# A long convolution by matrix steps: rows regrouped by residue, two steps of the second half in small tiles, their exchanges through DRAM

## The chip, the core and the metric

The program runs on one core of a Trainium2 chip. The core has five engines that run side by side, each working through its own instructions in order: PE (matrix products; the loading of its weights is listed apart as PEld), DVE (element by element), ACT (functions and casts), POOL (small work) and SP, which here only issues transfers. The transfers themselves are carried by 16 DMA engines. The metric is the time of one execution in device microseconds (us); lower is better.

## The reference

All matrices are bf16; S = 2048 rows, D = 512 columns. The core of it:

```
x  = q
k_shift[t] = k[t]*s0 + k[t-1]*s1 + k[t-2]*s2 + k[t-3]*s3      (per column)
kv = k_shift * v
y  = causal convolution of kv with ssm_k over the 2048 rows    (by a Fourier transform of length 4096)
h  = x + layernorm(x) * (y + kv * ssm_D)
z  = layernorm(h)
g  = gelu(layernorm(z) @ w1), its four quarters of columns moved by -1, +1, -2, +2 rows
x1 = z + g @ w2
out = h + x1 + gelu(layernorm(x1) @ w3) @ w4                   (hidden width 1792)
```

## The kernel before

**Layout.** Row t of the sequence is t = 1024 s + 8 p + b: half s, partition p (0 to 127), block b (0 to 7). A block is a 128 x 512 tile, a pair is two blocks. So a load of q or v reads, for each of 128 partitions, one contiguous piece of several rows.

**The convolution.** The two halves of kv are called A0 and A1, those of the filter F0 and F1. Each goes through a transform in two steps. Step 1 (tasks S1, L397) multiplies 128 x 512 blocks by a 128 x 32 table `f1`; of each table only a quarter of the rows is nonzero (the mask `mk`, L238), so that one product picks out one residue of the row number. There are four b by two hp tasks of 8 products for each of the four signals. The result in PSUM is cast to SBUF (E1, L266), and an exchange (X, L412) moves it between partitions, SBUF to SBUF: 8 transfers of 256 KB for each signal. Step 2 (S2, L420) is followed by a cast (E2, L266); for F1 the place of the cast is taken by a fold on DVE (L432), which joins F1's spectrum with F0's (16 instructions). Products of spectra (P, L481) go through the inverse's first step (I2, L493, 32 x 32 tiles), a cast (EV, L266), an exchange (XI, L503, four transfers of 512 KB for each half) and the inverse's last step (I1, L511), with a table `f2` that is masked in the same way. The first half needs A0 F0; the second A0 F1 + A1 F0. The shift of k is done by products with diagonal tiles (K, L449), the gating with v on DVE (KV, L457).

**After the convolution.** H (L619) forms h from I1, HS takes its moments, uw, rr and hn turn them into scales, hb (L653, L655) normalizes. hb is transposed per pair either on PE (LT, L671, with a copy TE) or through DRAM by a transfer that transposes (LT L664, TE L666; `BYDMA` lists the pairs). W (L700) is w1, U the gelu (L704), X2 (L729) w2 on shifted blocks, S (L732) x1, R (L736) the residual. Then come ux, r1, xn and lb, the transpose (LX, EX), M (L781, w3, seven tasks of 16 products a pair), G (L785, gelu), O (L793, w4, 14 products a block), Z (L795, the sum into `obt`, two slots) and OUT (L797).

**Order.** `Plan` records some 800 tasks; nothing is scheduled on the chip. The string `ORDER` lists them by number, engine letter and buffer slots, and each engine runs its tasks in that order; so a task that waits holds all that stands behind it on its engine. Every transfer is issued by SP. The built program uses eight completion semaphores for them in turn: a transfer waits until the one eight places before it has landed. SP issues 125 transfers. All but one have 128, 64 or 32 as the outermost count on both sides; the one is `Lsd` (L280), a single row.

**Memory.** `fxs` (the filter) lies in `r_h`, q in `r_q`, v in `r_v`; `r_x`, `r_y`, `r_f0`, `r_f1`, `r_a0` hold spectra and later the hidden activations.

Of the kernel before, what the change touches and what calls it, by code (L numbers as in the profile page):

```python
# [9 lines left out]
P = 128  # L10
S = 2048
D = 512
F = 1792
DC = D // P
FC = F // P
NB = 8
XW = 258
KW = NB * 129 + 4
# [13 lines left out]
029P7 004S 030P 031V 067P01 069P23 005S 033A 068A 041V 042G 070A 003S 037V 008S 036V 040V 063P45 002S 064A 065P67 066A 059P01 046V 099P30 043V 000S  # L32
060A 047V 001S 007S 006S 034G 038A 032V 044V 035G 105P2 010S 100V 091P71 061P01 039A 055P45 106V 009S 048A 021S 092V 056A 340V 101P6 102V 103P3 104V
045A 062A 097P2 098V 015S 022S 342V 023S 343V 093P7 057P45 019S 053G 119P01 058A 120A 095P6 049G 050V 121P23 051A 094V 054G 017S 122A 115P45 117P01
118A 024S 078S 096V 111P67 113P23 114A 116V 107P45 112V 109P01 110A 108V 074S 088P6723 090V 089A 345V 077S 071S 073S 075S 085P0145 087V 079P6723 127S
086A 130S 128S 123S 081A 344V 219P10 220V 080A 131P2345 133A 132V 124S 134P6701 135V 136A 072S 076S 082P2345 083A 084A 223P1 125S 144V0 129S 137P6723
020S 227P01 138A 143V1 146V2 147V3 139A 145P45670 148P 231P3 224V 149M 150A 228V 346V 152V0 012S 126S 187P01 189P45 188A 190A 153V1 155V2 018S 232V
014S 195P67 011S 183P01 196V 185P23 184A 186V 013S 191P45 192A 151S 025S 156V3 140P6701 142A 141A 154P23451 157P 347V 225P1 016S 197P67 158M 159A 198A
221P0 201S 161V0 162V1 226V 199S 200S 193P23 194A 341V 163P45670 202S 348G 165V2 164V3 166P 168A 167A 222V 160S 233P1 204S 229P0 170V0 171V1 174V2
239P23 173V3 203S 349G 172P45671 234V 240A 175P 230V 177A 176V 350G 354G0 207P0123 052A 208V 206S 209V 235P67 216P4501 217V 236A 351G1 241P67 242A  # L40
271V0 169S 339G 205S 243P23 244A 178S 179P54 218V 237P67 238A 355V 360G0 247P23 336S 352V 357G1 335S 180P10 361V 358V 356A 338S 245P67 248A 353A 375V
249P45 181P03 246A 366G0 367V 250A 182P12 255S 363G1 251S 364V 376G 377V 362A 359A 372G0 365A 252S 213P4567 215V 378A0 369G1 379P30 381A1 373V 374A
026S 027S 382P2 380A 370V 272V1 259P6701 254S 383A 260A 388G 389G 390G 214V 274V2 275V3 258S 386P3 371A 387A 210P4567 212V 211V 256S 261A 273P01230
391A0 392P71 394A1 395P6 276P 277V0 413G 414G 393A 396A 368A 278V1 262P4567 281V2 415G 401G 253S 402G 403G 280V3 263A 028S 279P 257S 282P 283M 284A
416V0 399P5 400A 384P4 385A 418S 417V1 419S 286V0 268P0123 420S0 264V 269A 397P7 398A 287V1 289V2 270V 404G0 290V3 265P4501 266A 288P23671 291P 406S
423P5 405A1 292V0 424A 293V1 296V2 267A 294P 421P4 295V3 297P 422A 285S 298A 407S 513P5 302V0 301V1 303P01230 304V2 408S0 305V3 306P 299A 509P4 514V
307V0 308V1 411P5 515A 409P7 510V 511A 310V2 311V3 309P 312P 412A 317V0 410A 521P7 313A 300S 314A 517P6 316V1 320V2 319V3 318P01451 522V 321P 322V0
525P3 337S 573G 574G 575G 579A0 576A1 323V1 325V2 577P70 578A 529P2 580P7 315S 326V3 523A 324P 581A 518V 519A 602G 603G 604G 605G0 327P 329A 328A
582P70 588P6 594P5 430V 431V 429V 584P4 426V 585A 330S 583A 425V 592P1 593A 586P0 427V 589A 587A 428V 432V 433V 590P4 591A 526V 530V 434G 527V 606A1
331P76 332P43 333P21 531A 435V 439G0 595A 516V 440V 599P5 436A1 441A 437V 445G0 442G1 630V 438V 446V 451A0 443V 608S 596P0 631G 632G 607S 609S0 600V0  # L50
601S 460G 461G 334P37 444A 447A 473G 452V 448A1 633V0 635S 610P60 614P1 634V1 611A 616P5 620P6 449V 612P4 450V 457G0 453V 454A1 618P2 615A 462G 466A0
613A 617A 458V 622P7 636S 637S1 638P10 644P5 623A 455V 463V1 464P70 465A 621A 459V 619A 524V 640P4 456V 467P3 645A 646P7 474G 475V 477G1 479S 468V
469P6 471P5 497V 520V 498G 624P3 476A0 499V 478S 528V 480S0 472A 470A 500A1 625V0 502S 533P6 534V 485G 501A0 503S 504S1 537P5 538V 648P3 650P6 649A
539A 535V 483P5 484A 486G 487V 642P3 643A 489V0 491S 481P2 647A 488G1 627P5 658G 659G 660G 482A 512V 597V1 532V 662A0 507P7 490S 492S0 641A 661A1 663S
508A 505P4 495P0 493P7 506A 541P4 545P3 626S 546V 639A 494A 496A 553P7 557P2 561P3 651A 549P6 547A 554V 542V 543A 742V 743G 562V 563A 598S 555A 558V
744V 745A1 550V 569P4 565P7 566V 664S 665S0 666P30 667A 674P2 675A 678P6 652P7 655P3 560V 746V0 748S 628V0 672P5 564V 629S 747S 749S1 676P2 570V 571V
750P40 751A 668P1 669A 548V 756P0 551V 757A 686G 687G 688V 677A 690V0 692S 752P4 753A 689V1 552V 673A 670P1 671A 559V 760P2 761A 762P5 691S 714V 715G
716V 754P4 718G0 717V1 693S0 758P2 759A 694P10 696P0 653V0 654S 704P7 719S 568V 679A 705A 680P2 700P7 540V 695A 536V 763A 702P6 698P5 755A 767P4 720S
656V1 567V 657S 699A 701A 770G 771G 697A 706P7 721S1 722P50 772G 773G0 730P3 774G1 731A 556V 776S 724P1 725A 544V 775S 683P0 684V0 777S0 734P3 703A
764P6 707A 778P70 784P1 685S 728P0 785A 735A 765V0 766S 711P6 681V1 782P1 572V 783A 712V0 713S 682S 732P3 733A 726P6 729A 768V0 769S 727A 708P2 709V1  # L60
710S 723A 788P6 789A 739P5 740V0 741S 790P6 786P4 791A 787A 780P5 781A 736P6 737V0 738S 779A 792P7 793V1 794S 795P6 796V0 797S
# [3 lines left out]
class Plan:  # L65
# [4 lines left out]
    def add(self, name, opts, fn, deps=(), take=(), drop=(), size=0, mode=0, port="", mate=None):  # L70
        n = len(self.t)
        t = dict(mate=mate, n=n, name=name, opts=opts, fn=fn, deps=set(), take=list(take), drop=[], size=size, mode=mode, port=port)
        for d in deps:
            t["deps"].add(self.by[d])
        for d, part, *kind in drop:
            m = self.by[d]
            t["deps"].add(m)
            t["drop"].append((m, kind[0] if kind else self.t[m]["take"][0][0], part))
        self.by[name] = n
        self.t.append(t)  # L80
# [20 lines left out]
def body(ctx, tc, fx, kt, q, v, sd, w1, w2, w3, w4, out):  # L101
# [13 lines left out]
    def view(raw_, lo, n, pat, **kw):  # L115
        return raw_[:, lo:lo + n].rearrange(pat, **kw)


    G = 8192
    GS = FC * 256  # L120
    r_q, r_f0, r_f1, r_a0, r_x, r_y, r_v = (raw(n, G) for n in ("r_q", "r_f0", "r_f1", "r_a0", "r_x", "r_y", "r_v"))
    r_k = raw("r_k", 2 * DC * KW)
    r_h = raw("r_h", DC * NB * XW)
    r_kv = raw("r_kv", 8 * D)
    r_p = raw("r_p", 4 * 2 * D)
    r_vs = raw("r_vs", 2 * 4 * D)
    r_dg = raw("r_dg", DC * 4 * P)
# [718 lines left out]
```

## Time and profile before

| | |
|---|---|
| timed executions | 220.81 and 221.84 us, median 221.32 |
| the profiled execution, first to last instruction | 221.2 us |
| PE, DVE, ACT, POOL busy | 200.6, 145.3, 134.9, 67.3 us |
| transfers | 34.47 MB, mean 156 GB/s |
| the first I1 of the first half (L511) starts | 56.2 us |
| the first step 2 of A1 (L420 on r_x) starts | 68.7 us |
| last product ends, last sum (Z) ends | 217.5, 218.2 us |

A table row here is a view's own number, or a start that stands in the timeline of one engine. Busy shares are means over the whole run: PE is busy 91% of the span, but what bounds the first third is not what bounds the rest, so the prediction reads the profile by stage. The page's own span and the median of the two timed executions differ by 0.1 us.

### The profile page before, as it was taken

To read this page: it belongs to the slowest core of one execution; us is meant where nothing else is said; L and a number is where in the kernel's file an instruction comes from. 1 tells how busy PE (TensorE), PEld (TensorE's weight loads), DVE (VectorE), ACT (ScalarE), POOL (GpSimd) and SP (SyncE) were. 2 spreads that over 40 slices of the span, in tenths; PEclk is the share of its full clock that TensorE was granted. 3 is DMA by queue.
4 is the path that set the end of the run, shared out by engine and by line. 5 is a ranking of instruction groups with operands and counts; after the bars stand their busy time and mean duration, and the time that the engine had idled before them with its cause. 6 is when DMAs were issued, how large, how long until landed. Compare 5 with 4: busy or idle time off the path is not lost.

```text
span 221.2 us, 5913 instructions
## 1 busy us (share of the span) xinstructions
PE 200.6 (91%) x2372; PEld 118.7 (54%) x2372; DVE 145.3 (66%) x320; ACT 134.9 (61%) x214; POOL 67.3 (30%) x187
## 2 busy tenths in 40 slices
PE   6889578996867799999999999999999999999993
PEld 4454234451223255558548958746588666665641
DVE  7898989999499899899899348059765001312121
ACT  4799889988498979687956646655063323123400
POOL 7342000093276680234685345003125000000000
PEclk9999999999695899999999999999999999999998
DMA  6996798869927535973234154341415402111001
GB/s 193 363 394 271 286 291 318 309 244 307 426 115 268 187 83 160 269 303 98 50 74 95 27 113 102 89 104 46 91 32 142 98 2 45 47 50 47 24 24 47
DMA packets 35996, 34.47 MB, mean 156 GB/s; under 512 B 26753, under 2 KB 28802, under 8 KB 35714
## 3 DMA queue, kind: packets, MB, share of 16 engines
q1 hardware_dynamic: 35970, 34.11, 48.6%
q8 instruction: 18, 0.29, 0.6%
q14 instruction: 8, 0.07, 0.1%
HBM read 13.13 MB, written 5.24 MB: 83 GB/s over the span
## 4 chain that ended last, share of the span: by engine, by line
PE 67%; DMA 11%; SPq 6%; ACT 6%; DVE 5%; issue 2%; POOL 0%; DVEq 0%
PE ps L781 22%; PE ps L793 22%; PE ps L729 6%; PE ps L700 5%; PE ps L493 4%; SPq L412 4%; DMA r_h<-in_fx_dram 3%; SPq L275 3%; DMA r_k<-in_kt_dram 3%; DMA r_x<-r_y 3%; PE ps L511 3%; DVE r_f L432 2%; PE ps L397 2%; ACT r_y L266 2%; DMA r_f<-r_y 2%
## 5 line engine op out<-in xcount | busy, mean ns | idle before, releaser
L781 PE MATMUL ps<-r_dg,r_k 128*128 128x256 bf16 x448 | 51.4, 273 | 0.0
L781 PEld LDWEIGHTS <-r_k 128*128 128x128 bf16 x448 | 43.6, 98 | 7.8 <-issue 0.7
L785 ACT ACTIVATE r_f<-ps 128x512 bf16<-128x512 f32 x26 | 14.9, 598 | 27.8 <-PE ps L781 27.8
L793 PE MATMUL ps<-w4s,r_f 128*128 128x512 bf16 x104 | 24.1, 379 | 0.0
L481 DVE TENSOR_TENSOR r_p<-r_a,r_f 128x1024 bf16<-128x1024 bf16 x32 | 20.8, 694 | 1.0 <-PE ps L493 0.9
L266 ACT CAST r_y<-ps 128x1024 bf16<-128x1024 f32 x19 | 18.6, 1022 | 4.6 <-PE ps L397 4.1
L493 PE MATMUL ps<-r_p,ttab 32*32 32x512 bf16 x768 | 15.8, 379 | 1.4 <-ACT r_x L266 0.6
L700 PE MATMUL ps<-hnT,r_v 128*128 128x256 bf16 x128 | 16.5, 281 | 0.5 <-DMA hnT<-dhb 0.5
L795 DVE TENSOR_TENSOR r_kv<-ps,r_v 128x512 bf16<-128x512 f32 x5 | 3.4, 686 | 20.5 <-PE ps L793 20.5
L795 DVE TENSOR_TENSOR r_kv<-ps,r_a 128x512 bf16<-128x512 f32 x6 | 4.2, 692 | 19.3 <-PE ps L793 17.3
L449 PE MATMUL ps<-r_dg,r_k 128*128 128x256 bf16 (+3 forms) x112 | 15.8, 288 | 1.0 <-ACT r_dg L314 0.5
L785 ACT ACTIVATE r_x<-ps 128x512 bf16<-128x512 f32 x16 | 9.2, 599 | 12.2 <-PE ps L781 12.2
L793 PEld LDWEIGHTS <-r_f 128*128 128x128 bf16 x104 | 10.2, 98 | 11.8
L266 ACT CAST r_vs<-ps 128x1024 bf16<-128x1024 f32 (+1 forms) x12 | 14.3, 1228 | 2.4 <-PE ps L493 1.9
L700 PEld LDWEIGHTS <-r_v 128*128 128x128 bf16 x128 | 12.5, 100 | 5.1 <-issue 2.0
L793 PE MATMUL ps<-w4s,r_x 128*128 128x512 bf16 x64 | 15.1, 379 | 0.0
L729 PE MATMUL ps<-r_v,r_h 128*128 128x512 bf16 x64 | 15.0, 380 | 0.0
L449 PEld LDWEIGHTS <-r_k 128*128 128x128 bf16 x112 | 9.5, 98 | 8.9 <-issue 4.6
L266 ACT CAST r_x<-ps 128x1024 bf16<-128x1024 f32 x14 | 13.7, 1017 | 0.7 <-PE ps L397 0.4
L397 PEld LDWEIGHTS <-f 128*32 128x32 bf16 x256 | 6.2, 99 | 12.6 <-issue 7.3
L493 PEld LDWEIGHTS <-ttab 32*32 32x32 bf16 x768 | 8.3, 88 | 8.7 <-issue 6.0
L793 PE MATMUL ps<-w4s,r_kv 128*128 128x512 bf16 x56 | 12.6, 379 | 0.0
(180 smaller groups left out, 343.8 us busy)
## 6 DMA issues: line engine op xcount, KB each, us to landing
r_k<-in_kt_dram SPq DMA_DIRECT2D x8, 259.0 KB, 5.6
r_h<-in_fx_dram SPq DMA_DIRECT2D x8, 256.0 KB, 4.9
r_v<-in_v_dram SPq DMA_DIRECT2D x4, 512.0 KB, 6.2
r_q<-in_q_dram SPq DMA_DIRECT2D x8, 256.0 KB, 6.4
r_f<-r_x SPq DMA_DIRECT2D x8, 256.0 KB, 3.0
r_a<-r_y SPq DMA_DIRECT2D x8, 256.0 KB, 3.5
r_x<-r_vs SPq DMA_DIRECT2D x4, 512.0 KB, 3.5
r_f<-r_y SPq DMA_DIRECT2D x8, 256.0 KB, 4.0
```

Of the source, the lines that this page charges most:

```text
L266: (act.copy if e in "AM" else on[e].tensor_copy)(o, i)
L397: nc.tensor.matmul(ps[32 * j:32 * j + 32, sl[hh], :], lhsT=f1t[:, 4 * t + 2 * hp + hh, :], rhs=src(2 * b + b0), start=True, stop=True)
L412: nc.sync.dma_start(z2[sig][g:P:2, kl, :, :], z1[sig][kl:P:4, 2 * g:2 * g + 2, :, :])
L449: nc.tensor.matmul(o[:, (d + j0) * P:(d + j1 + 1) * P], lhsT=kT[s][c][:, bb, x:x + P], rhs=diag[:, c, j0:j1 + 1, :].rearrange("p j x -> p ...
L481: on[e].tensor_tensor(out=prs[:, sl[0], :, :], in0=sp[a][:, kl, t, :, :], in1=gv, op=MUL)
L493: nc.tensor.matmul(ps[c:c + 32, bk[h], :], lhsT=ttab[32 * h:32 * h + 32, 2 * kl + t, 2 if x else xx, 32 * b0:32 * b0 + 32], rhs=prs[32 * h ...
L700: nc.tensor.matmul(ps[:, sl[0], j * 256:(j + 1) * 256], lhsT=w1s[:, k, m * P:(m + 1) * P], rhs=hnT[:, k_, k, :], start=(k == 0), stop=(k = ...
L729: nc.tensor.matmul(ps[:, sl[0], :], lhsT=h1T[:, m, bb, x:x + P], rhs=w2s[:, m, :], start=(m == 0), stop=(m == DC - 1))
L781: nc.tensor.matmul(ps[:, sl[0], j * 256:(j + 1) * 256], lhsT=w3s[:, k, fc * P:(fc + 1) * P], rhs=lnT[:, k_, k, :], start=(k == 0), stop=(k ...
L785: act.activation(gb(gi, 2 * fp, 2), ps[:, got(("M", s, p, fp))[0], :].rearrange("p (j x) -> p j x", j=2), ACT.Gelu_apprx_tanh)
L793: nc.tensor.matmul(ps[:, sl[0], :], lhsT=gb(gi, fc)[:, 0, (b % 2) * P:(b % 2 + 1) * P], rhs=w4s[:, fc, :], start=(fc == 0), stop=(fc == FC ...
L795: add(("Z", s, b), {V: 0.61}, lambda e, sl, b=b: vec.tensor_tensor(out=obt[sl[0]], in0=ps[:, got(("O", s, b))[0], :], in1=h_sb[s][:, b, :] ...
```

## The change

The rows keep their blocks, but within a block the 128 rows are regrouped by residue: partition 32 r + n now holds what partition 4 n + r held. Loads of q and v and the stores of the output therefore read and write DRAM with outermost count 4 and 32 rows under each. k and the filter are regrouped on the host.

With the residues apart, step 1 of F1 and A1 no longer needs a mask: a residue is 32 partitions, and the product is one of 32 x 32 tiles (`step1r`), four tasks of 16 products for A1, and four of 32 for F1, which takes over the fold: it adds F0 times a turned table `s1g`. The eight tasks of step 1 of F0 and A0 stay masked. The exchanges of F1 and A1 go through DRAM: 16 writes of 128 KB each (XW, outermost count 8) and then 4 reads of 512 KB (XR), the first of which waits for all 16 writes. The second half's last inverse step is unmasked too (64 x 32 tiles, `f2u`), and its exchange also goes through DRAM: 16 writes XIW and 4 reads XIR. SP issues 159 transfers.

The memory plan is new: F1's filter lies in the second half of `r_q`, so the q loads of the second half wait for F1's step 1, and so do w1 and w2; h overwrites v's place; Z writes in place, without slots; six buffers for hidden activations in place of four; shifted rows across the ends of a block get spare columns (`HO`, `KO`) and small copies (exa, exb, ed0, ed1, edge0, edge1). Pairs (0,2) and (0,3) of hb are transposed on PE. The first half's pairs go into M and O in the order (0,1), (0,2), (0,0), (0,3), and ORDER is new: two pairs' M stand among the second half's I2, and the second half's I1 stands behind the O of those two.

```diff
-KW = NB * 129 + 4
+KW = 5 * P + 3 * 160 + 4
...
 ORDER = """
...
-    for i in range(2):
-        for j in range(2):
-            vec.tensor_scalar(out=f1[:, :, i, :, j, :], in0=s1.rearrange("p (a c k) -> p a c k", a=8, c=2),
-                              scalar1=mk[:, 2 * i + j:2 * i + j + 1], scalar2=None, op0=MUL)
+    for r in range(4):
+        vec.tensor_scalar(out=f1[:, :, :, :, r, :].rearrange("p h t c k -> p (t c) h k"), in0=s1[:].rearrange("p t c (k h) -> p (t c) h k", h=4),
+                          scalar1=mk[:, r:r + 1], scalar2=None, op0=MUL)
...
-    v_r = v.rearrange("o (s p b) d -> p (o s) b d", s=2, b=NB)
-    q_r = q.rearrange("o (s p b) d -> p (o s) b d", s=2, b=NB)
-    o_r = out.rearrange("o (s p b) d -> p (o s) b d", s=2, b=NB)
+    v_r = v.rearrange("o (s n r b) d -> r n (o s) b d", s=2, r=4, b=NB)
+    q_r = q.rearrange("o (s n r b) d -> r n (o s) b d", s=2, r=4, b=NB)
+    o_r = out.rearrange("o (s n r b) d -> r n (o s) b d", s=2, r=4, b=NB)
...
-            load(("Lq", s, g), q_sb[:, s, 2 * g:2 * g + 2, :], q_r[:, s, 2 * g:2 * g + 2, :], size=310)
+            load(("Lq", s, g), q_sb[:, s, 2 * g:2 * g + 2, :], q_r[:, :, s, 2 * g:2 * g + 2, :], [("S1", "F1", b, 0) for b in range(4)] if s else [], size=310)
...
+    def step1r(b, srcs):
+        def f(e, sl):
+            for i, (src, tab) in enumerate(srcs):
+                for r in range(4):
+                    for t in range(2):
+                        for b0 in range(2):
+                            j = 2 * t + b0
+                            nc.tensor.matmul(ps[32 * j:32 * j + 32, sl[r], :], lhsT=tab[32 * r:32 * r + 32, 32 * t:32 * t + 32], rhs=src(2 * b + b0)[32 * r:32 * r + 32, :],
+                                             start=(i == 0), stop=(i == len(srcs) - 1))
+        return f
...
+    def forward1r(sig, srcs, sdeps, zdeps, xdeps, sdrop=None):
+        zd = scr.tile([P, 16, D], BF16, name="zd" + sig)
+        zx = zd[:].rearrange("(a r x) k d -> x r a k d", a=8, r=4)
+        for b in range(4):
+            n = ("S1", sig, b, 0)
+            add(n, {PEc: 0.23 * len(srcs)}, step1r(b, srcs), sdeps(b) + zdeps(b), take=[("ps", -2)], drop=[sdrop(b)] if sdrop else [], mode=3)
+            for hp in range(2):
...
+                def f(e, s, b=b, hp=hp):
+                    for r in (2 * hp, 2 * hp + 1):
+                        nc.sync.dma_start(zx[2 * (b % 2) + b // 2, r], z1[sig][:, b, r, :])
+                add(("XW", sig, b, hp), {SP: 0.85}, f, [("E1", sig, b, hp)], size=310)
+        for kl in range(4):
+            add(("XR", sig, kl), {SP: 0.6}, lambda e, s, kl=kl: nc.sync.dma_start(z2[sig][:, kl, :, :], zd[:, 4 * kl:4 * kl + 4, :]),
+                [("XW", sig, b, hp) for b in range(4) for hp in range(2)] + list(xdeps), size=620)
...
-                if sig == "F1":
-                    def fold(e, sl, n=n, kl=kl, t=t):
-                        for r, op in ((0, SUB), (1, ADD)):
-                            vec.tensor_tensor(out=sp[sig][:, kl, t, r, :], in0=ps[:, got(n)[2 * t + r], :], in1=sp["F0"][:, kl, t, 1 - r, :], op=op)
-                    add(("E2", sig, kl, t), {V: 1.2}, fold, [("E2", "F0", kl, t)], drop=[(n, t)])
-                    continue
...
+    wd = scr.tile([P, 16, D], BF16, name="wd")
+    wx = wd[:].rearrange("(a h k) n d -> k h a n d", a=8, h=4)
...
+            if s:
+                for hp in range(2):
+                    def f(e, sl, kl=kl, n=n, hp=hp):
+                        for h in (2 * hp, 2 * hp + 1):
+                            nc.sync.dma_start(wx[kl, h], vst[:, got(n, "vs")[0], h, :])
+                    add(("XIW", kl, hp), {SP: 0.85}, f, [("EV", s, kl, hp)], size=310, drop=[(n, 0, "vs")])
...
+        for b in range(4 if s else 0):
+            add(("XIR", b), {SP: 0.6}, lambda e, sl, b=b: nc.sync.dma_start(wv[1][:, :, b, :], wd[:].rearrange("p (r b) d -> b p r d", b=4)[b]),
...
+                    if s:
+                        nc.tensor.matmul(ps[32 * h:32 * h + 32, sl[b0], :], lhsT=f2u[r, :], rhs=wv[1][r, h, b, :], start=True, stop=True)
...
-        hd = [("KV", g, c) for g in (0, 1) for c in range(DC)] if s == 0 else allp(0)
+        hd = [("KV", 2 * s + g, c) for g in (0, 1) for c in range(DC)] + ([("O", 0, b) for g in (0, 2) for b in MLP[g]] if s else [])
...
-            add(("Z", s, b), {V: 0.61}, lambda e, sl, b=b: vec.tensor_tensor(out=obt[sl[0]], in0=ps[:, got(("O", s, b))[0], :], in1=h_sb[s][:, b, :], op=ADD),
-                [("R", s, b)], take=[("ob", 1)], drop=[(("O", s, b), 0)])
+            add(("Z", s, b), {V: 0.61}, lambda e, sl, b=b: vec.tensor_tensor(out=h_sb[s][:, b, :], in0=ps[:, got(("O", s, b))[0], :], in1=h_sb[s][:, b, :], op=ADD),
+                [("R", s, b)], drop=[(("O", s, b), 0)])
```

## The prediction

> **What bounds the kernel now.** I read the stages first: busy tenths in 40 slices of 5.5 us.
>
> ```profile
> PE   6889578996867799999999999999999999999993
> ...
> DVE  7898989999499899899899348059765001312121
> ...
> DMA  6996798869927535973234154341415402111001
> ```
>
> From slice 18 on (92 us and later) PE is full and nothing else is. Before that PE has gaps while DVE and the transfers are nearly full. The chain that ended last says the same in order of time (start, length, what):
>
> ```profile
> 4.31 5.59 DMA r_k<-in_kt_dram
> ...
> 46.67 3.73 DMA r_f<-r_y
> ...
> 56.19 1.89 PE ps L511 x8
> ...
> 64.72 2.59 DMA r_x<-r_y
> ...
> 106.40 2.70 PE ps L511 x24
> 109.09 6.15 PE ps L793 x28
> 115.24 0.97 PE ps L511 x8
> ...
> 208.42 9.08 PE ps L793 x42
> ```
>
> Up to about 92 us the chain hops between exchanges, DVE and ACT; then it is a row of products that all count in full. So the front is priced by what arrives last, the rear by the sum of products. Third, how full the 16 DMA engines are in two short stretches (the last two columns are their busy share and GB/s):
>
> ```profile
> 14.00:16.00 2.00, 2.00 (x19) 1.40 (x17) 1.51 (x3) 2.00 (x4) 1.77 (x5) 1.00 1.03 389
> ...
> 22.00:24.00 2.00, 1.16 (x32) 0.31 (x31) 2.00 (x3) 1.93 (x2) 0.00 (x0) 1.00 1.02 404
> ```
>
> All sixteen together are saturated at 404 GB/s, so one engine carries 404 / 16 / 1.02 = 24.8, by the first row 23.6; I use 24.5 GB/s. Last, two groups that the change touches (busy us, mean ns of one) and, from the list of transfers, size and median us from issue to landing:
>
> ```profile
> L432 DVE TENSOR_TENSOR r_f<-ps,r_f 128x512 bf16<-128x512 f32 x16 | 10.0, 681 | 1.1 <-issue 1.1
> ...
> L397 PE MATMUL ps<-r_kv,f 128*32 128x512 bf16 x128 | 9.1, 407 | 0.8 <-ACT r_y L266 0.6
> ```
>
> ```profile
> r_v<-in_v_dram SPq DMA_DIRECT2D x4, 512.0 KB, 6.2
> ...
> r_x<-r_y SPq DMA_DIRECT2D x8, 256.0 KB, 3.9
> ...
> dlb<-r_k SPq DMA_DIRECT2D x14, 128.0 KB, 2.1
> ```
>
> **PE.** Eight masked step 1 products take 0.55 us in a run (chain: 0.56, 0.55). F1 and A1 have 16 such tasks, 8.8 us. After: four tasks of 32 small products (a run of 32 such, L493, takes 0.58) and four of 16 (half, 0.3): 3.5. Saved 5.3, all before 62 us, where PE is not what is late. I1 of the second half costs 2.70 + 0.97 = 3.7 now; 64-row tiles of 32 columns (L420, 16 products in 0.63) give 4 x 0.35 = 1.4, saved 2.3 in the full stretch. Two more pairs' LT on PE add 4 x 0.22 = 0.9. **DVE** loses the fold, 10.0, and takes one of the eight casts that replace it (1.22); the other seven go to ACT (1.02 each); E1 of F1 and A1 moves three casts from ACT to DVE. Net DVE -5, ACT +4. Table building, edge copies and the ends of blocks are POOL and DVE work under 1 us each beside other work; if uncovered, 2 us in all. Z without slots frees one wait of 2.0 us on DVE, behind which only later Z stood: nothing. The order of pairs alone moves no product in or out: nothing, bounds -2 to +2 us. H of the second half now waits for four O; PE runs these 12 us of products anyway, and behind H on DVE stand only its successors.
>
> **Transfers.** SP issues 34 more. 48 writes at the 0.41 us of the nearest row (L664) and 12 reads at 0.55 replace 20 exchanges at 0.6 and six transposing ones (4.0): about +10 us of issuing, beside waits. What decides is how the new shapes spread. The trace keeps completion records of every transfer: sixteen for those with 128, 64 or 32 rows, but two for the one-row Lsd, the first at its issue, the second 3.7 us later. So the number of engines follows the shape; a transfer with an outermost count of 4 (q, v and the output, after) or 8 (XW, XIW) lies between 1 and 32. No row shows it. One end is 16 engines, the other one engine; I take one engine for each outermost step, 4 and 8, because the nearest shape on that side, one row, has one engine, and 32 rows over 16 engines divide evenly as 4 and 8 do only over themselves.
>
> [...]
>
> With 4 engines a load of 512 KB puts 131 KB on each: 131 / 24.5 = 5.35 us instead of 1.34; one of 256 KB 2.67 instead of 0.67. If such loads always meet on the same four (the costlier case, which I take: four that change from load to load would spread 3 MB over all), these carry everything in SP's order, and every transfer over 16 engines ends with its share on them. SP's window of eight keeps their queues filled throughout. The first eight loads end at about 9 us (windows: 1.9 MB moved by 8 us). Then v, v, q, q, v: 21.4, to 30.4. Two exchanges of F0: 31.7. v, q: 39.7. Seven transfers over 16 engines: 44.5. q: 47.2. Thirteen more, X of A0 among them: 56.0, landed (1.6 us of fixed time, 2.1 for 128 KB less its data) 57.6. Before, the last X of A0 was issued at 29.8 and landed after 3.5: 33.3. DVE waits in its queue too: Q.04 for a q load that lands at 41, with two E1 of A0 behind it, and Q.01 for the last one at 49, with the first products P behind it.
>
> From 57.6: S2 0.63, E2 1.22, four P of 0.69, I2 0.6, EV 1.22, XI 0.56 + 3.5: the first I1 at 68.1, not 56.2. After XI.03 is issued (64.1) the lowest eight engines carry XI 1.3, 16 writes of F1 at 16.4 KB / 24.5 = 0.67 (10.7), w1 1.3, 16 writes of A1 10.7, three XR of F1 4.0, w2 1.3, the first XR of A1 1.3: 30.7, with landing 97. So step 2 of A1 starts at 97, not 68.7. PE has only 8 us of products between, and idles.
>
> What stands in PE's order behind that step, at the rows' prices: 56 M and 12 W of 0.873, 16 O of 3.02, 16 X2 of 0.87, 16 I2 of 0.55, 5 S2, 7 transposes and I1 1.4: 136.2. The same count of before is 141.7, and it took 217.5 - 68.7 = 148.8, so 7.1 us of stalls; I keep half, 3.5, since DVE and ACT have caught up while PE waited. End of products: 97 + 136.2 + 3.5 = 236.7. After it Z, OUT and the end took 221.2 - 217.5 = 3.7; a store on 4 engines adds 1.0. Sum 241.4 us, I say 241. The span is 221.2, the median 221.32: no correction.
>
> **Rivals.** *All 16 engines carry the new shapes* (the faster side). Then the front is as before or better: DVE, over 95% busy from 20 to 56 us, loses 5 us, and the rear loses 2.3 less 0.9 of LT: 221.2 - 5 - 1.4 = 215, down to 208 if the 5.3 us of PE before 62 us count too. It decides as soon as the loads of q and v land in about 6 us as now. For it: every bulk transfer in the trace did reach 16; against it: the one-row record. *All 16, but the detour through DRAM is late*: a write of 128 KB lands after 2.1 and 16 issues take 6.6 us, then a read of 3.5 to 6.2; against 5 us of issuing and 3.9 the exchange of A1 comes some 5 us later, and the 5 us gained in the front are given back: 220. The inverse's exchange has 12 us of O before it. *Few engines, but partly covered*: the M of two pairs are fixed behind S2.A1 in PE's order, so PE cannot take them earlier; only a faster engine than 24.5 GB/s helps. At 27 the 88 us of the path scale by 0.9: 233.
>
> [...] The chain before has 64 small products, then 128-row ones at 92.81, 93.92 and 95.75 with no gap; no cost is taken.
>
> **Numbers.** Few engines 0.72 (own range 228 to 258), all 16 and faster 0.16 (208 to 216), all 16 and given back, or a mixture, 0.12 (217 to 226). The likeliest gives 241. The range 216 to 256 leaves out the fast rival and the upper tail. A difference under 2% (217 to 225.7) is about what a measurement of this kernel can't tell from none: faster 0.16, same 0.12, slower 0.72.
>
> **What would show it.** Right: q and v loads land after 10 us or more where they took 6; GB/s falls under 200 between 10 and 50 us while the DMA share is far below 1; the first I1 near 68 us, step 2 of A1 near 97, PE idle in slices 6 to 17 and full after; the same 136 us of products at the end; OUT landing near 3 us. Wrong: q and v landing in 6 us and the first I1 before 56 sinks the whole sum and leaves 215. First I1 near 68 but A1's step 2 near 80 means that the writes spread over all 16, and the end is near 225. Longer stalls after 97 than 3.5 us would put it above 245.

## The result, and the profile after

The changed kernel takes 270.91 us (two executions, 270.89 and 270.93) against 221.32: 1.2243 times the time before, 95% interval 1.2175 to 1.2311. The forecast was 241 in a range of 216 to 256, so the side was right and the size was not. The profiled execution spans 269.2 us; the sums below are made against that. Some executions of a kernel run over 1.5% longer than its shortest; the medians given here are of all executions, the ratios with an interval of the others alone.

The stages first: busy tenths in 40 slices, now of 6.7 us each.

```profile
PE   6756802778696038987999798998799999999980
...
DVE  6715405768999612775899742875486700020240
...
PEclk9968765778999555997999999999999999999996
DMA  7424554861665866993663647219344630010122
GB/s 216 176 105 153 175 174 158 302 217 62 222 216 201 288 242 216 263 329 133 183 278 86 152 119 234 81 43 178 95 99 97 137 81 2 0 37 5 39 60 76
```

The first third is no longer full. In slices 1 to 6 (7 to 47 us) DVE and PE have holes, and the transfers too are at half of their share or less, at 105 to 176 GB/s. The same two short stretches as before (columns: PE, PEld, DVE, ACT and POOL busy with their instructions, then PE's granted clock, DMA share, GB/s):

```profile
14.00:16.00 2.00, 0.00 (x0) 0.00 (x0) 0.17 (x1) 1.69 (x2) 0.43 (x2) 0.81 0.26 107
22.00:24.00 2.00, 2.00 (x16) 1.30 (x15) 0.26 (x1) 0.00 (x0) 0.00 (x0) 0.99 0.26 97
```

A share of 0.26 of 16 engines is four engines, and 107 GB/s over 0.26 x 16 is 25.7 GB/s for one. So four engines carry the regrouped loads at full pace, and twelve stand by. The completion records in the trace give the counts directly: a transfer with outermost count 4 leaves 5 of them, one with count 8 leaves 9, the single row 2 and all others 16 (28 x 5 + 48 x 9 + 2 + 82 x 16 = 1886, the number in the trace). The first of the 5, the 9 and the 2 comes right behind the issue (mostly 0.4 us after its end), as the prediction saw for the single row; the others, 4, 8 and 1, come with the data. The stretches showed 389 and 404 GB/s before. SP's own timeline (start, length, line, transfer, count) shows the queue that this makes:

```profile
6.70 4.88 SPq L271 DMA_DIRECT2D r_q<-in_q_dram  x2
11.62 5.23 SPq L271 DMA_DIRECT2D r_v<-in_v_dram  x1
16.98 3.23 SPq L432 DMA_DIRECT2D r_f<-r_f  x2
...
24.65 5.26 SPq L432 DMA_DIRECT2D r_f<-r_f  x2
```

One load held SP for 5.2 us while it was being issued (0.33 to 0.70 for the loads of q and v in the first experiment, where all 16 engines serve). The first exchanges of F0 are issued late, and they too have shares on the four full engines: of the 16 completion records of the one issued at 17.0 us, twelve come between 21.4 and 21.7 us, the other four between 30.7 and 33.3. What the front then waits for is DVE's own order:

```profile
43.15 0.69 DVE L559 BATCH_NORM_STATS2 qst<-r_q 128x6 f32<-128x512 bf16 x1 [13.20 <-DMA r_q<-in_q_dram]
...
56.29 2.49 DVE L513 TENSOR_TENSOR r_p<-r_a,r_f 128x1024 bf16<-128x1024 bf16 x4
...
62.19 2.50 DVE L513 TENSOR_TENSOR r_p<-r_a,r_f 128x1024 bf16<-128x1024 bf16 x4 [0.26 <-PE ps L525]
...
65.20 0.68 DVE L513 TENSOR_TENSOR r_p<-r_a,r_f 128x1024 bf16<-128x1024 bf16 x1
...
66.94 4.29 DVE L513 TENSOR_TENSOR r_p<-r_a,r_f 128x1024 bf16<-128x1024 bf16 x7
```

A statistic of q stands ahead of the casts of A0; it waits 13.2 us for its load, and the 16 products of spectra, casts and gatings queue up behind it. The chain of the work that ended last goes on like this:

```profile
68.74 2.50 DVE r_p L513 x4
...
77.45 1.04 PE ps L555 x8
...
93.12 6.57 DMA zdA<-r_z
99.71 6.02 DMA zdA<-r_z
106.78 9.27 DMA r_a<-zdA
...
162.55 5.10 DMA r_z<-wd
...
186.28 4.60 DMA r_dg<-dhb
```

The first I1 (L555) starts at 77.5 instead of 56.2; then the last writes of A1 and its second read, one after the other, stand in the chain for 22 us. That read was issued just behind a load of q for the second half, which again fills four engines: 12 of its 16 completion records come by 113.0 us, the other four at 115.6 to 116.0. A row of the chain is not PE's idle time, though: PE had other products meanwhile and waited 1.1 us for this read. Even behind 110 us the chain is no plain row of products any more. The new products are cheaper than the old ones; the inverse's last step is about as cheap as thought (1.6 us against 1.4), step 1 is not: A1's takes 3.1 us against 1.2 forecast (groups: count, busy us, mean ns; idle before), F1's 3.2 against 2.3.

```profile
L416 PE MATMUL ps<-r_kv,s 32*32 32x512 bf16 x64 | 3.1, 426 | 2.8 <-ACT r_z L262 2.5 <-DVE r_v L669 0.3
...
L553 PE MATMUL ps<-r_z,f2u 64*32 64x512 bf16 x32 | 1.6, 386 | 1.2 <-DMA r_z<-wd 1.1
```

### The profile page after: what moved, and what is told of

It reads as the page before. It is cut to its first block, busy times and chain, and to the rows that moved or that the text cites. A ratio compares the mean times of both kernels' runs of the same rounds, so it can differ in the third digit from the quotient of the medians.

```text
span 269.2 us, 6110 instructions
## 1 busy us (share of the span) xinstructions
PE 208.9 (78%) x2452; PEld 120.6 (45%) x2452; DVE 144.9 (54%) x336; ACT 136.5 (51%) x218; POOL 67.4 (25%) x181
## 4 chain that ended last, share of the span: by engine, by line
PE 38%; DMA 16%; ACT 10%; issue 3%; SPq 3%; DVE 3%; POOL 0%; ACTq 0%; DVEq 0%
PE ps L823 13%; PE ps L836 11%; PE ps L771 5%; DMA zdA<-r_z 5%; DMA r_a<-zdA 3%; PE ps L525 3%; DMA r_dg<-dlb 2%; ACT junk L653 2%; PE ps L750 2%; DMA r_z<-wd 2%; DVE r_p L513 2%; DMA r_dg<-dhb 2%; ACT r_z L262 2%; ACT r_vs L262 1%; SPq L538 1%
## 5 line engine op out<-in xcount | busy, mean ns | idle before, releaser
L823 PE MATMUL ps<-r_dg,r_k 128*128 128x256 bf16 x280 | 32.9, 273 | 2.1 <-DMA r_dg<-dlb 2.1
L838 DVE TENSOR_TENSOR r_v<-ps,r_v 128x512 bf16<-128x512 f32 x16 | 10.7, 686 | 42.9 <-PE ps L836 41.2
L262 ACT CAST r_f<-ps 128x1024 bf16<-128x1024 f32 (+1 forms) x19 | 19.3, 1060 | 26.7 <-DMA r_a<-r_a 11.8
L262 ACT CAST r_a<-ps 128x1024 bf16<-128x1024 f32 x23 | 22.4, 1020 | 6.3 <-PE ps L457 4.2
L457 PE MATMUL ps<-r_f,ftab 64*32 64x512 bf16 x128 | 7.6, 553 | 22.3 <-DVE r_a L262 11.7
L823 PE MATMUL ps<-xtx,r_k 128*128 128x256 bf16 x168 | 20.0, 273 | 0.0
L559 DVE BATCH_NORM_STATS2 qst<-r_q 128x6 f32<-128x512 bf16 x16 | 10.8, 685 | 15.5 <-DMA r_q<-in_q_dram 15.5
L487 DVE TENSOR_TENSOR r_kv<-ps,r_v 128x512 bf16<-128x512 f32 x16 | 10.7, 683 | 12.5 <-DMA r_v<-in_v_dram 7.6
L669 DVE SCALAR_TENSOR_TENSOR r_v<-ps,qsd,z_t 128x512 bf16<-128x512 f32 x16 | 11.7, 743 | 9.0 <-PE ps L553 8.2
L774 DVE SCALAR_TENSOR_TENSOR r_q<-r_v,hrr,ps 128x512 bf16<-128x512 bf16 x16 | 11.7, 745 | 7.8 <-PE ps L771 7.5
L750 PEld LDWEIGHTS <-r_fx 128*128 128x128 bf16 x128 | 12.6, 103 | 7.1 <-DMA r_dg<-dhb 2.3
L750 PE MATMUL ps<-r_dg,r_fx 128*128 128x256 bf16 x96 | 12.9, 290 | 1.8 <-DMA r_dg<-dhb 1.8
```

The costliest lines, as they stand in the source:

```text
L262: (act.copy if e in "AM" else on[e].tensor_copy)(o, i)
L457: nc.tensor.matmul(ps[32 * h:32 * h + 32, sl[2 * t + r], :], lhsT=ftab[64 * t:64 * t + 64, 4 * kl + h, r, :], rhs=z2[sig][64 * t:64 * t + ...
L559: return lambda e, sl: vec.bn_stats(qst[:, 8 * s + b, :], q_sb[:, s, b, :])
L669: vec.scalar_tensor_tensor(out=h_sb[s][:, b, :], in0=ps[:, got(("I1", s, b // 2))[b % 2], :], scalar=qsd[:, i:i + 1], in1=z_t[:, got(("Y", ...
L750: nc.tensor.matmul(ps[:, sl[0], j * 256:(j + 1) * 256], lhsT=w1s[:, k, m * P:(m + 1) * P], rhs=xt[:, k, :], start=(k == 0), stop=(k == DC ...
L774: vec.scalar_tensor_tensor(out=q_sb[:, s, b, :], in0=h_sb[s][:, b, :], scalar=hrr[:, 4 * s + b // 2, 0, b % 2:b % 2 + 1], in1=ps[:, got((" ...
```

## Experiments

All stand against the kernel before on the same chip (medians 221.36, 220.42 and 220.88 in three sessions). The runs with the loads alone, "loads regrouped" and "before, few-engine loads", have one execution each. Stages of the profiled executions, in us, read from PE's timeline:

| kernel | first I1 | step 2 of A1 | last product ends | span | timed median |
|---|---|---|---|---|---|
| before | 56.2 | 68.7 | 217.5 | 221.2 | 221.3 |
| after | 77.5 | 109.8 | 261.4 | 269.2 | 270.9 |
| loads regrouped | 51.2 | 84.4 | 232.0 | 239.7 | 241.5 |
| and stores | 51.8 | 84.5 | 231.7 | 235.3 | 238.4 |
| and writes | 53.0 | 83.0 | 226.4 | 229.9 | 230.1 |
| before, few-engine loads | 80.3 | 92.7 | 245.7 | 249.3 | 251.1 |
| loads in 32 rows | 59.2 | 93.2 | 242.4 | 250.2 | 254.9 |
| joined writes | 51.3 | 78.4 | 221.0 | 224.7 | 226.9 |
| base, plain reads | 51.6 | 80.6 | 223.2 | 226.7 | 229.1 |
| direct exchange | 52.6 | 76.9 | 219.1 | 222.7 | 224.9 |
| 32 neighbouring rows | 57.3 | 90.2 | 236.7 | 244.6 | 251.2 |
| after, writes alone | 77.2 | 106.9 | 250.7 | 258.2 | 258.5 |

### Loads, stores and writes, one after the other

The first three give back 16 engines to one kind of transfer each, the host doing the regrouping that k and the filter already have.

```diff
-    v_r = v.rearrange("o (s n r b) d -> r n (o s) b d", s=2, r=4, b=NB)
-    q_r = q.rearrange("o (s n r b) d -> r n (o s) b d", s=2, r=4, b=NB)
+    v_r = v.rearrange("o (s p b) d -> p (o s) b d", s=2, b=NB)      # q_r alike; rows of q, v regrouped on the host
```

> The changed kernel, but q and v are regrouped on the host, so that each load is 128 rows in DRAM again. Theory (a transfer runs on as many engines as its outermost count allows, and what queues behind it on these engines waits): the loads land in about 6 us, DMA share and GB/s rise together again, the first I1 comes at 52 to 57 us instead of 77, step 2 of A1 some 31 us later (the exchange writes still run on 8 engines), at 84 to 88 instead of 110; time about 240 us (235 to 248) against 270.9. Rival (the loads are hidden; the detour through DRAM and the new order are the cause): first I1 comes earlier but the time stays above 260 us.

Measured 241.49 us: 29.4 us of the 49.6 are the loads of q and v. The first I1 is at 51.2, 5 us ahead of before, which fits the 5 us that the fold's removal takes from DVE, though no run parts that. The same stretch as above, two us earlier, shows all engines at work:

```profile
12.00:14.00 2.00, 2.00 (x26) 1.02 (x25) 1.93 (x5) 1.45 (x3) 2.00 (x5) 1.00 1.04 414
```

Next, the stores are written as 128 rows too (the host puts the rows back):

```diff
-    o_r = out.rearrange("o (s n r b) d -> r n (o s) b d", s=2, r=4, b=NB)
+    o_r = out.rearrange("o (s p b) d -> p (o s) b d", s=2, b=NB)
```

> As e1, and the output is stored as 128 rows too and regrouped on the host. Theory: after the last product 261.4 to 269.2 = 7.8 us passed in the changed kernel and 3.7 in the one before; the stores on 4 engines queue up, so this run ends 3 to 4 us before e1: about 236. Rival (the end waits for something else): same time as e1 within 1 us.

Measured 238.36 (236.34 to 240.04), ratio to before 1.0774 (1.067 to 1.0879). The time behind the last product falls from 7.7 to 3.6 us; nothing ahead of it moves by more than 0.6. The stage shows the gain; the medians alone (241.49 of one execution, 238.36 of four that spread over 3.7 us) would not.

Third, the 48 writes to DRAM:

```diff
-                        nc.sync.dma_start(zx[2 * (b % 2) + b // 2, r], z1[sig][:, b, r, :])
+                        nc.sync.dma_start(zp[4 * (2 * (b % 2) + b // 2) + r], z1[sig][:, b, r, :])   # zp: 16 runs of 128 rows; XIW alike
```

> As e2, and the 48 exchange writes to DRAM go to 128 consecutive rows each (all engines) instead of 8 x 16; the data land in other places, so F1's, A1's and the second inverse's values are not the convolution's, while every transfer keeps its size and every wait its place. Theory: 32 writes at 0.67 us become bound by the issue at 0.4 to 0.57, the exchange of F1 and A1 shortens by 4 to 10 us, the time falls to about 228 (220 to 234). Rival (latency of the detour and the wait for all 16 writes, not the engines): within 3 us of e2.

Measured 230.14 (229.43 to 231.7), ratio 1.0422 (1.0355 to 1.0488): 8.2 us by the medians, 5.4 between the two profiled executions (235.3 to 229.9), of which 2.7 in the stage from I1 to step 2 of A1 (4 to 10 were expected there) and 3.8 behind it, less 1.2 ahead of it. The edit changes the addresses in DRAM together with the count; for the writes these two were not parted. The trace now has 158 x 16 + 2 = 2530 completion records. With 16 engines everywhere the new kernel is still 8.8 us slower than before, so "few engines" explains 40.8 of the 49.6 us and not all. In its chain:

```profile
59.53 5.30 DMA r_fx<-in_w_dram
64.84 5.42 DMA r_f<-zdF
...
128.81 5.48 DMA r_z<-wd
```

### The loads alone, on the kernel before

```diff
-    v_r = v.rearrange("o (s p b) d -> p (o s) b d", s=2, b=NB)
+    v_r = v.rearrange("o (s n r b) d -> r n (o s) b d", s=2, r=4, b=NB)      # q_r alike
```

> The kernel before, with one thing of the change: its loads of q and v take the rows by residue (4 x 32), nothing else is regrouped, so the rows it works on do not match k and the output is not the reference's. Theory: these loads take 5.3 and 2.7 us on 4 engines, the first I1 comes at 70 to 78 us instead of 56, the time goes from 221 to 235 to 245 us. Rival (loads are hidden): under 226 us.

Measured 251.11: 29.75 us above before, more than expected, and the same as what the loads cost in the changed kernel (29.4). The price is the loads' own and needs nothing else of the change. SP's timeline, first the exchanges of F0 in the kernel before, then this run:

```profile
12.33 8.70 SPq L412 DMA_DIRECT2D r_f<-r_x  x6
```

```profile
6.85 4.24 SPq L275 DMA_DIRECT2D r_k<-in_kt_dram  x1
11.14 6.12 SPq L275 DMA_DIRECT2D r_q<-in_q_dram  x2
...
23.62 13.20 SPq L412 DMA_DIRECT2D r_f<-r_x  x6
```

The row of six exchanges of F0, all 16-engine transfers, is 13.2 us long instead of 8.7 (both rows contain a pause of some 5 us; the issues in them last 7.6 us together instead of 3.6), and one k load takes 4.2 us to issue: with a queue on the few engines, what used them as well was held here, at SP already.

### Is it the count or the addresses?

```diff
-            load(("Lq", s, g), q_sb[:, s, 2 * g:2 * g + 2, :], q_r[:, :, s, 2 * g:2 * g + 2, :], ...)
+            for r in ...: nc.sync.dma_start(q_sb[32 * r:32 * r + 32, s, ...], q_r[r, :, s, ...])     # v alike; same addresses
```

> The kernel after, with its twelve loads of q and v each cut by residue into transfers of 32 rows (24 in all, of 128 or 256 KB); addresses, regrouping and everything else stay as they are. Theory (the outermost count of a transfer sets how many engines carry it): 32 rows spread over 16 engines, so this does what the host's regrouping of q and v did in the first experiment (241.5 us): first I1 near 51, S2 of A1 near 85, and with 12 more issues of some 0.45 us, partly beside waits, 241 to 246. Rival (the regrouped rows themselves cost: each partition reads a piece of DRAM that lies far from its neighbour's): the addresses are unchanged, so 262 to 271.

Measured 254.88 (252.38 to 257.52), between the two: 16 us better than after at the same addresses, so the count acts; but 13 us worse than loads of 128 rows. First I1 at 59.2, not 51. The pieces also hold other blocks than the loads that they replace: each of v has a quarter of the partitions of all eight blocks, so a block is complete only with the last of four. How much of the 13 us that has was not parted. In the stretch of 12 to 14 us:

```profile
12.00:14.00 2.00, 1.18 (x18) 0.34 (x16) 0.88 (x2) 1.40 (x3) 2.00 (x4) 1.00 0.94 204
```

Now 0.94 of 16 engines are busy, and they move 204 GB/s, 13.6 GB/s for each. The rate itself has two possible causes: the rows' distance in DRAM slows them, or that each transfer fills only 32 partitions. A second run reads neighbouring rows. It leaves the transposition out of ten reads behind 110 us, as does a base for this and the next runs:

```diff
-        ... nc.sync.dma_start_transpose(xT[sl[0]]..., d[:].rearrange("c p x -> (c p) x"))
+        ... nc.sync.dma_start(xT[sl[0]]..., d[:].rearrange("c (g r) x -> (c g) (r x)", r=8))
```

> A base for the next runs: the third experiment's kernel (all transfers over 16 engines, 230.1 us) with its ten transposing reads replaced by plain reads of the same 256 KB, so that these blocks reach the products untransposed. All of them stand behind 110 us in its order, so the first I1 (53.0) and S2 of A1 (83.0) should stay within 1 us; behind them a plain read is issued in some 0.5 us instead of 1.2 and lands sooner than the 3 us of the chain's four waits for them, so 224 to 229 us if those waits shorten, 230 if something else is late just behind.

Base: 229.06 (228.29 to 230.0), ratio 1.0373 (1.0327 to 1.0419), 1.1 us less than with transposing reads; step 2 of A1 at 80.6 was expected within 1 us of 83.0 and is 2.4 earlier, though nothing ahead of it was edited, so a profiled execution's stage is good to a few us only.

> The loads cut into 24 transfers of 32 rows (254.9 us), but from rows regrouped on the host, so that each transfer reads one run of neighbouring rows of DRAM; the transposing reads are plain ones, as in the base. In the run before all 16 engines were busy from 10 to 25 us (share 1.02 to 1.06) and moved only 215 to 238 GB/s, where 128-row loads moved 388 at the same share. Theory A (a transfer that fills only 32 partitions is slow on the side of the partitions): the first I1 stays at 58 to 60 us, and 10 to 25 us show 215 to 240 GB/s at full share. Theory B (the rows' distance in DRAM makes it slow): the first I1 at 51 to 54 us, as with 128-row loads from regrouped rows, and over 330 GB/s between 10 and 15 us. The end is 2 to 6 us lower by the plain reads in either case: 249 to 253 by A, 237 to 243 by B. [...]

Measured 246.71, 247.29, 255.06 and 255.81; the first of these is the profiled one, with the first I1 at 57.3 and

```profile
12.00:14.00 2.00, 1.18 (x18) 0.34 (x16) 0.93 (x2) 2.00 (x4) 2.00 (x5) 1.00 0.96 204
```

The rate is the same 204 GB/s from neighbouring rows. For the rate theory A holds: from neighbouring rows it is 202, 204 and 264 GB/s between 10 and 16 us, from distant ones 228, 204 and 267, while 128 partitions got 381 and 414 between 10 and 14. By the times the case is less clean. The first I1 lies between the two theories, 1.9 us ahead of the run with distant rows, and so do the two shorter executions (247.0 us); these are 7 us below that run's three shorter ones (252.4 to 255.6), where the plain reads brought 1.1 us in the base. So the rows' distance may cost a few us more, outside the stretch shown. Why loads into 32 partitions ran at half the rate no run shows.

### The writes alone, on the kernel after

The third edit above, without the first two, and plain reads.

> The kernel after (270.9 us) with its 48 writes to DRAM spread over 16 engines, to 128 consecutive rows each (data elsewhere than the reference needs), and plain reads for the transposing ones as in the base; loads and stores as in after. Read by stage: in after the first I1 starts at 77.5 and S2 of A1 32.4 us later; beside regrouped loads the same edit of the writes shortened that stage from 32.7 to 30.0. Theory (the writes have their own price, whatever the loads do): first I1 at 77 to 78, S2 of A1 29 to 31 us later, the end 6 to 9 us less by the writes and 2 to 6 by the plain reads, 256 to 263. Rival (the queues of the few engines, still full with q and v, hide it): the stage stays at 32 or more and the end is 265 to 269. The prediction's sum would halve 21.4 us of engine time in that stage: 22 us.

Measured 258.54 (255.13, 257.59, 259.49 and 259.96), within the theory's range; the stages are those of the longest of the four. The stage from I1 to step 2 of A1 is 29.7 us instead of 32.4, the rest (step 2 of A1 to the last product) 143.7 instead of 151.5. So the writes have a price of their own, whatever the loads do: 12.4 us are gone by the medians, 14.6 by the two shorter executions, 1.1 of them by the plain reads if these count here as in the base. The first I1 stays at 77.2; the loads set it. That the stage would shrink with the engines' time, to 22 us, is refuted: spreading the writes won 2.7 us there and not 10.7. Most of their price shows further back, 7.8 us behind step 2 of A1; which of XIW, the later reads and the transposes has it was not parted.

### What remains with 16 engines

Joined writes, 24 of 256 KB instead of 48 of 128:

```diff
-                    for r in (2 * hp, 2 * hp + 1):
-                        nc.sync.dma_start(zp[...], z1[sig][:, b, r, :])
+                    nc.sync.dma_start(zp[2 * (2 * (b % 2) + b // 2) + hp], z1[sig][:, b, 2 * hp:2 * hp + 2, :])    # XIW alike
```

> The third experiment's kernel (all transfers over 16 engines, 230.1 us) with each two writes of 128 KB to DRAM joined in one of 256 KB: 16 writes XW and 8 XIW in place of 32 and 16; as there, the data land in other places than the reference needs. Theory A (what remains against the kernel before, 8.8 us, is SP issuing 48 writes): 16 XW stand in a row ahead of step 2 of A1 on its path, 0.5 us each in its trace, so some 8 us go: S2 of A1 at 75 to 77 instead of 83.0, end at 222 to 225. Theory B (what remains is the two passes through DRAM, write landing 5.3 us and read landing 5.4 us, each waited for in full): larger writes land no sooner, S2 of A1 stays at 80 to 83 and the end at 227 to 230.

Measured 226.93 (226.45 to 228.43), ratio 1.0298 (1.0219 to 1.0376): 3.2 us less, or 2.3 if each run is taken against its own session's before (8.8 and 6.5 above it). The end lies on B's side, step 2 of A1 at 78.4 between both. SP's timeline, base first, then joined:

```profile
48.58 9.52 SPq L446 DMA_DIRECT2D zdF<-r_a  x16
```

```profile
48.01 6.66 SPq L445 DMA_DIRECT2D zdF<-r_a  x8
```

Half the issues took 6.7 us instead of 9.5, so joining saves less than the count suggests. It is not that a larger write takes longer to issue: in both rows the shortest issues last about 0.4 us (0.43 for 256 KB, 0.32 to 0.45 for 128 KB). Both rows contain a few long ones, up to 1.67 and 1.27 us; what held these was not looked into.

Then the exchanges of F1 and A1 made directly, SBUF to SBUF, as before. The first try issued each at the second block in number of its pair:

```diff
+                    for kl in (2 * hp, 2 * hp + 1) if b % 2 else ():
+                        nc.sync.dma_start(z2[sig][b // 2:P:2, kl, :, :], z1[sig][kl:P:4, b - 1:b + 1, :, :])   # no XW, no XR
```

> The third experiment's kernel with the exchanges of F1 and A1 made as in the kernel before, SBUF to SBUF in eight transfers of 256 KB each, at the place of the writes in the order, and no pass through DRAM for them (the data land in other places than the reference needs, so this is a price and not a remedy; the inverse's exchange still goes through DRAM). Theory (the detour through DRAM carries what remains): S2 of A1 at 69 to 73 instead of 83.0, as before's 68.7, and with the 5.5 us fewer products behind it 217 to 221 in all. Rival (the new order of front work, casts and weight loads, carries it): S2 of A1 stays above 78 and the end above 226.

> As the experiment with direct exchanges of F1 and A1, and the exchange of the second half's inverse too made as before, four transfers of 512 KB from SBUF to SBUF in place of 16 writes and 4 reads of DRAM (again the data land elsewhere than the reference needs). Theory (the rear stalls between 98 and 134 us in the third experiment belong to the inverse's writes and reads, 5.5 us of them at the read alone): 2 to 5 us less than with the first detour alone undone, near 215. Rival (they belong to the transposes through DRAM and to the casts): the same time as with the first detour alone undone, within 1 us.

Measured 242.29 (241.38 to 243.04) and 241.84 (241.01 to 244.07). The first run's stage matches the rival's figure, but not for its reason. The order handles block 1 before block 0, so the exchange was issued ahead of a cast into its source, and the cast waited for it (ACT's timeline; in brackets the idle time and what ended it):

```profile
58.12 1.01 ACT L262 CAST r_a<-ps 128x1024 bf16<-128x1024 f32 x1 [9.18 <-DMA r_f<-r_a]
```

That is a wait of the edit's own making, and the run tells nothing of the detour. Between the two, the inverse's detour shows no difference, as its rival had it; no run prices it in a kernel without that wait. Issued behind the last cast of each pair:

```diff
+                    g = {("F1", 2, 0): 1, ("F1", 0, 0): 0, ("A1", 0, 0): 0, ("A1", 3, 0): 1}.get((sig, b, hp))
+                    for kl in range(4) if g is not None else ():
+                        nc.sync.dma_start(z2[sig][g:P:2, kl, :, :], z1[sig][kl:P:4, 2 * g:2 * g + 2, :, :])
```

> The first try at direct exchanges (242.3 us) issued them too early in the program: the second block of each pair was still to be cast, and that cast then waited for the exchange to read the old content (ACT idle from 49 to 58 us, with the exchange r_f<-r_a named), so it priced a wait of its own making. Here the four exchanges of a pair of blocks are issued behind the pair's last cast, as the kernel before does it; otherwise it is the base with plain reads, and F1 and A1 make no pass through DRAM (their data land elsewhere than the reference needs). Theory (the detour through DRAM carries what remains of the front): the casts of A1 end at 66 us as in the third experiment, four issues of 0.6 and a landing of 3.9 put S2 of A1 at 73 to 77 instead of 83.0, and the end 6 to 10 us under the base. Rival (the new order of casts, weight loads and products carries it): S2 of A1 above 80, the end within 3 us of the base.

Measured 224.93 (224.12 to 227.0), ratio 1.0198 (1.014 to 1.0257), 4.1 us under the base, short of the theory's 6 to 10 and more than the rival's 3; the stages give the same, 219.1 against 223.2, and step 2 of A1 at 76.9 lies in the theory's range. Against before it is slower by 1.4 to 2.6%. PE's timeline around step 2, base first:

```profile
68.90 1.91 PE L457 MATMUL ps<-r_f,ftab 64*32 64x512 bf16 x32 [6.50 <-DMA r_f<-zdF]
...
80.59 0.62 PE L457 MATMUL ps<-r_a,ftab 64*32 64x512 bf16 x16
```

```profile
65.23 1.96 PE L458 MATMUL ps<-r_f,ftab 64*32 64x512 bf16 x32 [1.87 <-ACT r_z L262]
...
76.91 0.63 PE L458 MATMUL ps<-r_a,ftab 64*32 64x512 bf16 x16
```

The wait of 6.5 us for the read of F1 is gone, and 1.9 for a cast takes its place. From step 2 of F1 to that of A1 it is 11.7 us in both: in that stage PE's order, with transposes and four W between, decides and not A1's exchange. So of the 8.2 us that the base is above before, the detour of F1 and A1 has 4.1. For the other 4 no run stands, and in the profiled executions only 1.5 of them show (222.7 against 221.2, where other executions of before span 218.2 to 220.3). Step 2 of A1 is still 8.2 us later than before, 11.8 us more behind the first I1 (24.3 against 12.5), while the way from there to the end is 6.6 us shorter (142.2 against 148.8); that it is the new order of casts, H and step 1 is read from the chain, where DVE's H and casts fill 52 to 64 us, and was only argued.

## Why the prediction was wrong

**The cause, right.** Four engines carried the loads and stores and eight the writes, as many as their outermost counts, as the completion records show (4 and 8 with the data); that loads of count 4 always meet on the same four is what the records of the exchange of F0 show, twelve early and four late. That the eight are the lowest of the 16, as the sum has it, no run shows; the records show in its place that they hold the loads' four: of the write issued at 119.7 us, behind loads of q whose last record comes at 134.3, four shares land by 128.1 and the other four between 134.1 and 134.9. The rate of one engine fits too (24.5 taken, 25.7 in the stretch shown). The rivals with 16 engines fall. The regrouped loads carried 29.4 us, the largest part, and "few engines" 40.8 of 49.6 us in all.

**The loads' transfers, nearly right; what follows them, too small.** The sum of queues put the landing of the last exchange of A0 at 57.6; it was issued at 54.5 to 55.0, against 56.0 in the sum, and its last completion record is at 59.7. The first step that failed is "From 57.6 ... four P of 0.69": beyond the four products of spectra then running, DVE had twelve more ahead of it, with a statistic, two gatings and three casts: 12 x 0.62 + 0.7 + 2 x 0.7 + 3 x 1.22 = 13.2 us of work that its wait for q had pushed back. PE, which works in order too, shows where this enters: the last step 2 of A0, put at 57.6, stands behind two runs of I2, which need DVE's products.

```profile
61.06 1.93 PE L525 MATMUL ps<-r_p,ttab 32*32 32x512 bf16 x64
...
63.92 1.44 PE L525 MATMUL ps<-r_p,ttab 32*32 32x512 bf16 x64
65.29 0.62 PE L457 MATMUL ps<-r_a,ftab 64*32 64x512 bf16 x16
```

It starts 7.7 us late; from there to the first I1 it is 12.2 us instead of 10.5. So the first I1 came at 77.5, not 68.1: 9.4 us. The landing was 2 us off; the work behind it was counted from the last exchange only.

**The stage of the writes, nearly right, but only in part for its reason.** 28.9 us were forecast from first I1 to step 2 of A1, 32.4 measured. The queue on eight engines is real: by the completion records the writes land 0.64 to 0.74 us apart where nothing lies between (0.67 taken), the last of A1 at 105.7, and its first read at 109.8, when step 2 starts. But PE's row of products between step 2 of F1 and that of A1 ends at 109.8 as well. Engine time alone didn't set the stage: with the writes on 16 engines it is still 29.7 (30.0 in the third experiment). With the writes alone spread, step 2 of F1 comes 16.9 us behind the first I1 instead of 20.2, and the way from it to that of A1, in PE's order, is 12.9 instead of 12.2. SP's issuing (0.7 us a write of F1 with its waits), the casts and PE's order stand close behind the queue; that the sum of the queue alone came near is in part luck.

**Stalls in the rear, too small: the largest miss.** 3.5 us were taken, half of before's 7.1; 151.5 - 136.2 = 15.3 measured. "DVE and ACT have caught up" was wrong. Two things are in the 15.3. PE is busy 141.6 of the 151.5 us, 5.4 more than the rows' prices give, as it was before (146.5 against 141.7); and it is idle 9.9 us, where before it was 2.3. Its longest waits there are those for transposed blocks (`r_dg`, 2.1 and 1.8), for the inverse's read and for A1's second read (1.1 each), and 2.0 that the profile gives no releaser. Regrouped loads and stores bring the stalls to 11.0 (231.7 - 84.5 - 136.2), 16-engine writes to 7.2 (143.4 - 136.2), as many as before had, with PE idle for 6.7 and 4.1 us. So what the rear stalls beyond before's belongs to the few engines, whose effect the sum ended at step 2 of A1, but for one store; which transfer has how much was not parted. The inverse's exchange was held to be covered by 12 us of O, and nearly was: its read stands in the chain even with 16 engines (128.81, 5.48 us), but PE waited 0.2 us for it there and 1.1 in after.

**The end, too small.** 4.7 us were taken for one store on four engines; 7.8 measured, 3.5 with 16. SP issues seven stores between 256.2 and 262.7, each 128 / (4 x 24.5) = 1.3 us, and they stand in line: their last completion records lie 1.35 to 1.7 us apart, the last at 268.2.

Together: 9.4 + 3.5 (32.4 - 28.9) + 11.8 + 3.1 = 27.8, which is 269.2 - 241.4. All four misses go one way: a queue was priced by its own length, and what it makes late next was not. **The gain in PE's part was right:** 5.5 us fewer products behind step 2 of A1 (136.2 against 141.7; PE's busy time there is 139.3 in the third experiment against 146.5), and that gain shows in the runs with 16 engines, where the way from step 2 of A1 to the last product is 5 to 7 us shorter than before. Some readings of the kernel before were loose without moving the sum by more than 0.3 us: PE's row is at nine tenths or more from slice 14 on (counted from 0; 77 us), not from 92, DVE is busy 94% from 20 to 56 us, not over 95%, the last exchange of A0 lands at 35.2 by its records, not 33.3, and the rows listed for the 136.2 add up to 136.5.

## What to carry to other kernels

Before a layout is changed, look at the outermost count of every transfer that touches it, on both sides: 4 instead of 128 in the loads cost 29 to 30 us here in either kernel, and cutting the loads into pieces that fill 32 partitions each gave back only 16 of them; in the stretch shown their rate was half, 204 GB/s against 414. When a transfer becomes late, list all that stands behind the waiting instruction in its engine's order and add that up, not only the chain from the transfer. The pass of F1 and A1 through DRAM in place of direct exchanges cost 4.1 us here, with a wait of 6.5 us for its read; the smaller products of step 1, some 3 us less work in a stage where PE idles, did not pay for it.

## What was not expected of the hardware

- A few full engines held the issuer: behind loads that only four engines carry, single issues on SP took up to 5.2 us, and four of the 16 shares of an exchange landed 9 to 12 us behind the other twelve.
- All 16 engines can be busy at half the rate: 204 GB/s at shares of 0.94 and 0.96 with loads into 32 partitions, 414 at 1.04 into 128.
- PE's granted clock in the page's row falls to 0.5 in slices 13 to 15 (counted from 0), where PE first idles and then works again (0, 3 and 8 tenths), and the mean is 0.89 in after. A step 2 of 16 products takes 1.06 us there (103.5) and 0.62 later (116.1). Whether that cost time on the path was not tried.
